# Early-slot transposes three steps later, and early weight splits queued behind the routing of tile 5

## The chip, the cores and the metric

One core of a Trainium2 chip. The metric is the device time of one execution in microseconds (us). Engines are named TensorE (PE), VectorE (DVE), ScalarE (ACT), GpSimd (POOL) and SyncE (SP), as in the profile.

## The reference

Causal attention over 2 x 12 heads of 448 tokens, then a dense feed-forward layer with squared ReLU, then a top-1 mixture of 8 experts:

```python
x = attention(q, k, v)                      # (896, 768)
h = np.maximum(x @ w_in, 0.0); y = h * h @ w_out
yn = y / (norm(y) + 1e-6); en = emb / (norm(emb) + 1e-6)
logits = yn @ en.T / tau; idx = argmax(logits); gate_w = softmax(logits)[idx]
for e in range(8):
    mask = idx == e
    out[mask] = gate_w[mask, None] * (np.maximum(y[mask] @ w1[e], 0) @ w2[e])
```

Everything is float32. A product is made from three: each operand is split in a high part (ScalarE's copy, `mh`, `hi`) and a low part (VectorE's subtraction, `ml`, `lo`), both in a type that TensorE takes at full rate, and high x high, high x low and low x high are added up.

## The kernel before

The program runs in stages: attention; the first dense layer; the second dense layer (`b_tiles`, L484), tile by tile over seven tiles of 128 tokens, with 16 steps `f` each (`wo[f]`, six products of 384 columns); then the experts in *slots*. TensorE's order is written out by hand (`manual_schedule`, L871): work that belongs elsewhere hangs as hooks on steps. The other engines' orders come from a scheduler that goes by priorities; `urgent` (L853) raises the priority of what it wraps.

While tile t runs, its hooks route tile t-1 (`route_tile`, L508). Its parts are separated by `yield`, one per hook: transposes `yt` and their split `yhl`; the logit products `lgt` (two parts); the transposes `lg` of the logits (L535), from which VectorE takes a chain of small operations on 128x8 elements (L542 to L553) to the one-hot mask `OH`; then the rank product `rk` (L556), which reads `OH`. For tile 5, routed during tile 6, `rt6` hangs the parts on steps 1, 4, 7, 9 and 15.

The expert that is most frequent in the first five tiles is known early, and the *early slot* begins with its weights: 16 rows of tiles, loaded in 8 pieces (`pieces`, L663) of two, each split by ScalarE (`mh`) and VectorE (`ml`). Row k overwrites the place of `wo[k]`, so its `mh` waits until TensorE is through with step k of tile 6. The pieces are hooks of tile 6 (`hooks[-1]`): L489 makes one on every even step from 2 on; `all_of(ewl)` (L900) makes the last. Two gathered blocks of early tokens (`xr`) are transposed on steps 10 to 13 (`xe`; `xt`, L837), four groups of three; each group goes to a buffer of the PSUM pool `ps_h` (three buffers, L433, shared with `yt` and the products `hps`) and is emptied by a ScalarE cast (L841) and VectorE's subtraction `act<-xt`.

The early slot then runs `mm1` (8 steps of 18 products, `hps`) and `mm2` for its two halves of 128 tokens (8 steps of six products each, `ops`, L793). Through them goes one more iterator, `first()` (L1055): the routing of tile 6, the tables of all later slots (`tables`, ending in `tabp` and the row indices `fgi`), the gathers of the rows of the next slot M (POOL, L827), and the three groups of transposes of those rows: 128 tokens in two groups, then the remaining 32 tokens in one. `ft0`, `ft1`, `ft2` (L1064) say on which steps of `mm1`, of half 0 and of half 1 it advances. Slot M uses the early slot's weights.

Of the kernel before, what the change touches and what calls it, by code (L numbers as in the profile page):

```python
# [13 lines left out]
ALU = mybir.AluOpType  # L14
# [18 lines left out]
def f32(ap):  # L33
    return ap.bitcast(F32)


CFG = dict(
    first=1, rt5=[1, 3, 4, 5, 8], hp=3000, xe=[1, 10, 11, 12, 13], turn=5, xfd=[3, 4, 5, 6], xfj=[1, 2, 3, 4],
    joint=1, mhi="A", rt6=[1, 4, 7, 9, 15], woh="A", h2h="A", h2l="V", rt=[1, 3, 5, 7, 10], et=[9, 10, 14],
    turn2=[1, 3], ft0=[0, 1, 2, 3, 4], ft1=[3, 7], ft2=[2, 4, 5, 6], stop=0, mlo="V", xh="A", h2="A",  # L40
    wh="G", wil="G", wol="GV", warm=6, nsa=6, nwi=3, nwb=3, wo0=4, hs0=[4, 5, 8, 9], conv0=17, convs=2, pin=1,
    qsb=2, pb=2, ptb=2, qkraw=3, vraw=2, vb=2, ss=4, pts=3, pvs=1, pas=4, wsp=1, mz="G",
    seq=("p0 s0 n0 t0 v0 s1 v1 s2 t1", "n0 t2 s0 v2 v3 t3 s1 s2 w0"),
    ch=(((2, 0, 1), (3,), ()), ((6,), (4, 5), ())), wn=[1], qh="A", qdir=1, qss=2, rpin=5, qdma="SS", kh="V",
    vh="AG", kl="G", vl="G", pth="AAAA", nrm="GGGGGGG", u0=1, order=[2, 1, 3, 0, 4])


def build(tc, qkd, vd, w_in, w_out, emb, tau, wm, cst, out, dbg_y=None):
    nc = tc.nc
    V, A, G, T, DMA = nc.vector, nc.scalar, nc.gpsimd, nc.tensor, nc.sync  # L50
# [14 lines left out]
    def lo_of(eng, lo, x, hi):  # L65
        eng.tensor_tensor(out=lo, in0=x, in1=hi, op=ALU.subtract)  # L66
# [18 lines left out]
    c_tok1, c_im8, c_col, c_lane, c_kc, c_zi, c_ze, c_cap = (  # L85
        c_[k] for k in ("tok1", "im8", "col", "lane", "kc", "zi", "ze", "cap"))
# [42 lines left out]
    last = {}  # L129
# [239 lines left out]
    for p in (ps_v, ps_t, ps_s):  # L369
# [4 lines left out]
    h2 = [h2a_pool.tile([P, NF, GT], F32, tag="h2", name="h2_0"),  # L374
          h2b_pool.tile([P, NF, GT], F32, tag="h2", name="h2_1")]
# [33 lines left out]
    def more_h2():  # L409
        if chunks:  # L410
            c = chunks.pop(0)
            hsd[c] = h2_split(*c)
# [35 lines left out]
    def norm_of(pool, ss, n, name):  # L448

        r = pool.tile([P, 1], F32, tag="nr", name=name + "r")  # L450
        t = pool.tile([P, 1], F32, tag="nt", name=name + "t")
        V.tensor_scalar(out=r[:n].bitcast(I32), in0=ss.bitcast(I32), scalar1=1, scalar2=None,
                        op0=ALU.logical_shift_right)
        V.tensor_scalar(out=r[:n].bitcast(I32), in0=r[:n].bitcast(I32), scalar1=-1.0, scalar2=float(0x5F3759DF),
                        op0=ALU.mult, op1=ALU.add)
        for _ in range(3):
            V.scalar_tensor_tensor(out=t[:n], in0=r[:n], scalar=ss, in1=r[:n], op0=ALU.mult, op1=ALU.mult)
            V.tensor_scalar(out=t[:n], in0=t[:n], scalar1=-0.5, scalar2=1.5, op0=ALU.mult, op1=ALU.add)
            V.tensor_tensor(out=r[:n], in0=r[:n], in1=t[:n], op=ALU.mult)
        V.tensor_tensor(out=t[:n], in0=r[:n], in1=ss, op=ALU.mult)  # L460
        return t

    es = rpool.tile([E, 1], F32, name="es")
# [13 lines left out]
    OH = rpool.tile([P, NTI, E], BF16, name="OH")  # L477
# [6 lines left out]
    def b_tiles(ts, hooks={}):  # L484
        ps = {t: [ps_y.tile([P, 512], F32, tag=f"y{c}", name="yps") for c in range(2)] for t in ts}
        for f in range(NF):
            for x in hooks.get(f, ()):
                next(x, None)
            if f and f % 2 == 0 and -1 in hooks:  # L489
                next(hooks[-1], None)  # L490
            wh, wl = wo[f]
            for t in ts:
                hi, lo = (hsd[t, f // 4][:, i, f % 4, :] for i in range(2))
                for x, w in ((hi, wh), (hi, wl), (lo, wh)):
                    for c in range(2):
                        T.matmul(ps[t][c][:, :384], x, w[:, c * 384:(c + 1) * 384],  # L496
                                 start=(f == 0 and w is wh and x is hi), stop=(f == NF - 1 and x is lo))
            if f % 4 == 3:
                for t in ts:
                    more_h2()  # L500
        ys = {}
        for t in ts:
            ys[t] = bpool.tile([P, DM], F32, tag="ysb", bufs=2, name="ysb")
            for c in range(2):
                A.copy(ys[t][:, c * 384:(c + 1) * 384], ps[t][c][:, :384])
        return ys

    def route_tile(t, y):  # L508
        p0 = t * P
        DMA.dma_start(out=ydram[p0:p0 + P, :], in_=y)  # L510
        lgt = ps_r.tile([2 * E, 2 * P], F32, tag="lg", name="lgt")
        ytt = []
        for c in range(2):
            yt = ps_h.tile([P, 512], F32, tag="h", name="yt")[:, :384].rearrange("p (a b) -> p a b", b=P)
            for j in range(3):
                kc = 3 * c + j
                T.transpose(yt[:, j], y[:, kc * P:(kc + 1) * P], ident)
            ytt.append(yt)
        ss = rpool.tile([P, 1], F32, tag="ss", bufs=2, name="ss")
        sq = spool.tile([P, DM], BF16, tag="relu", name="sq")  # L520
        A.activation(sq, y, AF.Square, accum_out=ss)
        for c in range(2):
            yhl = bpool.tile([P, 3, 2, P], F32R, tag="yhl", name="yhl")
            A.copy(yhl[:, :, 0], ytt[c])
            lo_of(V, yhl[:, :, 1], ytt[c], f32(yhl[:, :, 0]))
            yield
            for j in range(3):
                kc = 3 * c + j
                T.matmul(lgt, ent[:, kc], yhl[:, j].rearrange("p a b -> p (a b)"), start=(kc == 0), stop=(kc == KC - 1))
        lgs = spool.tile([2 * E, 2, P], F32, tag="relu", name="lgs")  # L530
        V.tensor_copy(lgs, lgt.rearrange("p (a b) -> p a b", a=2))
        yield
        lg = ps_r.tile([P, 2, 2 * E], F32, tag="lg", name="lg")
        for j in range(2):
            T.transpose(lg[:, j], lgs[:, j], ident[:2 * E, :2 * E])  # L535
        nrm = norm_of(rpool, ss, P, "yn")
        sc = rpool.tile([P, 1], F32, tag="sc", bufs=2, name="sc")
        V.tensor_scalar(out=sc, in0=nrm, scalar1=1.0e-6, scalar2=None, op0=ALU.add)
        V.reciprocal(sc, sc)
        V.tensor_tensor(out=sc, in0=sc, in1=rtau, op=ALU.mult)  # L540
        l = rpool.tile([P, E], F32, tag="l", bufs=2, name="l")
        V.reduce_sum(out=l, in_=lg.rearrange("p j (a b) -> p b (j a)", b=E), axis=AX.X)  # L542
        V.tensor_scalar(out=l, in0=l, scalar1=sc, scalar2=None, op0=ALU.mult)
        m = rpool.tile([P, 4], F32, tag="m", bufs=2, name="m")
        V.reduce_max(out=m[:, 0:1], in_=l, axis=AX.X)
        V.tensor_scalar(out=m[:, 1:2], in0=m[:, 0:1], scalar1=-1.0, scalar2=None, op0=ALU.mult)
        ex = rpool.tile([P, E], F32, tag="ex", bufs=2, name="ex")
        A.activation(ex, l, AF.Exp, bias=m[:, 1:2], accum_out=m[:, 2:3])

        c8 = rpool.tile([P, E], F32, tag="c8", bufs=2, name="c8")  # L550
        V.scalar_tensor_tensor(out=c8, in0=l, scalar=m[:, 0:1], in1=c_im8, op0=ALU.is_ge, op1=ALU.mult)
        V.tensor_reduce(out=m[:, 3:4], in_=c8, op=ALU.min, axis=AX.X)
        V.tensor_scalar(out=OH[:, t], in0=c_im8, scalar1=m[:, 3:4], scalar2=None, op0=ALU.is_equal)  # L553
        yield
        rk = ps_r.tile([P, E], F32, tag="lg", name="rk")
        T.matmul(rk, tri, OH[:, t], start=True, stop=False)  # L556
        T.matmul(rk, ones, OHs[:, t], start=False, stop=True)
        V.tensor_tensor(out=OHs[:, t + 1], in0=OHs[:, t], in1=OH[:, t], op=ALU.add)

        g = rpool.tile([P, 1], F32, tag="g", bufs=2, name="g")  # L560
        V.tensor_scalar(out=g, in0=m[:, 2:3], scalar1=1.0e-9, scalar2=None, op0=ALU.add)
        V.reciprocal(g, g)
        gh = rpool.tile([P, 1], F32R, tag="gh", bufs=2, name="gh")
        V.tensor_copy(gh, g)
        V.tensor_copy(vals[:, t, 1:2], f32(gh))
        V.tensor_tensor(out=vals[:, t, 2:3], in0=g, in1=f32(gh), op=ALU.subtract)

        V.tensor_tensor(out=c8, in0=rk, in1=OH[:, t], op=ALU.mult)
        V.reduce_sum(out=ranks[:, t:t + 1], in_=c8, axis=AX.X)
# [306 lines left out]
    for t in range(2, NTI):  # L876
        hooks = {}
# [8 lines left out]
        if t == NTI - 1:  # L886
# [4 lines left out]
            ew, ewl = slot_w(eslot)  # L891
# [172 lines left out]
    for i, at in enumerate((CFG["ft0"], CFG["ft1"], CFG["ft2"])):  # L1064
        hooks = {k: [it] for k in at}
# [110 lines left out]
```

## Time and profile before

| | us |
|---|---|
| median of 3 runs | 589.86 |
| lowest, highest | 587.77, 589.89 |
| the profiled execution, its own time | 592.21 |
| its span, first to last instruction | 590.5 |
| TensorE busy in the span | 562.6 (95%) |
| VectorE, ScalarE, GpSimd busy | 399.0, 291.8, 192.3 |
| mean granted TensorE clock | 0.974 of 2.4 GHz |

The span leaves out 1.7 us of the execution around it. Times of rows count from the span's start. A matmul's duration in a row includes the overlap with its neighbours, so the pace of a run of matmuls is read from the starts of the rows.

### The profile page before, as it was taken

The page shows a single profiled execution, that of the slowest core. Times are in us where ns is not written, and L with a number is a line of the kernel's source. Part 1 is how long each engine was busy: PE and PEld are TensorE (multiplying, and loading weights), DVE is VectorE, ACT ScalarE, POOL GpSimd, SP SyncE. Part 2 cuts the span into 40 slices and gives each one's busy share as a digit, 9 for nine tenths or more (in the row PEclk, how much of TensorE's full clock was granted, in tenths as well). Part 3 has the DMA queues.
Part 4 walks back from the last instruction along what each step waited for, and adds up shares of the span by engine and source line. Part 5 has one row for each costly group of instructions (what it writes and reads, how often), then busy time and mean ns, then how long its engine had stood idle before and what let it go on. Part 6 is the DMA issues. An engine that isn't in the chain of part 4 may idle for free.

```text
span 590.5 us, 9782 instructions
## 1 busy us (share of the span) xinstructions
PE 562.6 (95%) x3501; PEld 516.5 (87%) x3501; DVE 399.0 (68%) x901; ACT 291.8 (49%) x654; POOL 192.3 (33%) x204
## 2 busy tenths in 40 slices
PE   6999999999999999999999999797998999899994
PEld 4888788889999999999899999797997788799993
DVE  6878688955687977796654459773187986942741
ACT  4778677523434244425233318511277976823651
POOL 7685667845446543211000010001202711500010
PEclk8899999999999999999999999799999999799998
DMA  7658442323435545341000039006677997950310
GB/s 223 169 144 233 115 99 68 109 85 114 161 123 176 197 162 178 131 175 55 1 27 28 28 110 394 33 1 221 227 221 244 318 340 241 339 182 21 116 44 9
DMA packets 28233, 86.51 MB, mean 147 GB/s; under 512 B 2822, under 2 KB 13062, under 8 KB 28176
## 3 DMA queue, kind: packets, MB, share of 16 engines
q1 hardware_dynamic: 26640, 79.51, 41.4%
q0 software_dynamic: 1536, 6.29, 3.1%
q8 instruction: 29, 0.48, 0.3%
q14 instruction: 28, 0.23, 0.1%
HBM read 75.24 MB, written 6.29 MB: 138 GB/s over the span
## 4 chain that ended last, share of the span: by engine, by line
PE 85%; DVE 6%; DMA 3%; ACT 3%; issue 2%; SPq 0%; POOL 0%; POOLq 0%; DVEq 0%; ACTq 0%
PE yps L496 19%; PE ops L793 9%; PE pa L289 7%; PE pa L290 7%; PE pa L288 7%; PE pv L264 6%; PE s L215 6%; PE pt L247 4%; PE hps L703 3%; DVE ml L66 3%; PE hps L719 2%; PE hps L718 2%; PE ops L735 2%; PE hps L720 2%; PE ops L730 2%
## 5 line engine op out<-in xcount | busy, mean ns | idle before, releaser
L66 DVE TENSOR_TENSOR ml<-xraw,mh 128x768 fp32r<-128x768 f32 x64 | 60.2, 951 | 19.2 <-ACT mh L59 19.0
L59 ACT ACTIVATE mh<-xraw 128x768 fp32r<-128x768 f32 x64 | 53.4, 845 | 19.0 <-PE ops L730 9.9
L215 PE MATMUL s<-kh,q 128*128 128x128 f32 (+6 forms) x168 | 53.4, 352 | 4.4 <-ACT p L219 4.3
L793 PE MATMUL ops<-mh,act 128*128 128x384 f32 x224 | 54.5, 347 | 0.0
L815 POOL DMA_INDIRECT out<-osb,fsi x10 | 24.3, 2433 | 85.5 <-ACT osb L810 63.9
L230 POOL TENSOR_SCALAR p<-p,rs 128x192 f32<-128x192 f32 (+6 forms) x84 | 44.3, 549 | 18.1 <-ACT p L219 11.3
L264 PE MATMUL pv<-pt,v 128*128 128x448 f32 (+7 forms) x288 | 48.6, 303 | 0.2 <-DVE pt L66 0.2
L827 POOL DMA_INDIRECT xr<-ydram,fgi x10 | 14.7, 1467 | 92.3 <-DVE fsi L605 49.8
L219 ACT ACTIVATE p<-s,mn 128x192 f32<-128x192 f32 (+6 forms) x84 | 39.6, 476 | 10.3 <-DVE mn L218 6.0
L123 DVE SCALAR_TENSOR_TENSOR w<-raw,w 128x768 int32<-128x768 int32 x32 | 42.8, 1338 | 0.7
L264 PEld LDWEIGHTS pv<-pt,v 128*128 128x128 f32 (+3 forms) x288 | 36.9, 163 | 5.4 <-issue 0.3
L215 PEld LDWEIGHTS s<-kh,q 128*128 128x128 f32 x168 | 35.4, 215 | 6.5 <-ACT p L219 4.9
L793 PEld LDWEIGHTS ops<-mh,act 128*128 128x128 f32 x224 | 40.2, 192 | 0.8
L66 DVE TENSOR_TENSOR ml<-mraw,mh 128x768 fp32r<-128x768 f32 x32 | 30.1, 950 | 14.8 <-ACT mh L59 14.8
L66 DVE TENSOR_TENSOR hs<-h,hs 128x512 fp32r<-128x512 f32 (+1 forms) x32 | 21.8, 690 | 24.8 <-ACT hs L59 24.6
L218 DVE TENSOR_REDUCE mn<-s 128x1 f32<-128x192 f32 (+6 forms) x84 | 34.1, 413 | 5.0 <-PE s L216 4.6
L121 DVE SCALAR_TENSOR_TENSOR w<-raw,w 128x768 int32<-128x768 int32 x32 | 36.0, 1128 | 0.7
L294 ACT ACTIVATE relu<-pa 128x448 f32<-128x448 f32 x32 | 17.1, 539 | 36.5 <-PE pa L290 36.2
L119 DVE TENSOR_SCALAR w<-raw 128x768 int32<-128x768 int32 x32 | 22.2, 694 | 18.0 <-POOL wi3l L66 6.7
L66 DVE TENSOR_TENSOR pt<-pt 128x512 fp32r<-128x512 f32 x48 | 32.3, 677 | 3.1 <-ACT pt L59 3.1
L247 PE MATMUL pt<-ident,p 128*128 128x128 f32 x192 | 32.1, 284 | 0.0
L59 ACT ACTIVATE mh<-mraw 128x768 fp32r<-128x768 f32 x32 | 26.7, 844 | 9.5 <-PE ops L793 3.7
(457 smaller groups left out, 1664.9 us busy)
## 6 DMA issues: line engine op xcount, KB each, us to landing
xraw<-in_wm SPq DMA_DIRECT2D x32, 768.0 KB, 5.9
raw<-in_w_in SPq DMA_DIRECT2D x16, 768.0 KB, 4.2
raw<-in_w_out SPq DMA_DIRECT2D x16, 768.0 KB, 4.2
mraw<-in_wm SPq DMA_DIRECT2D x16, 768.0 KB, 6.2
qk<-in_qkd SPq DMA_DIRECT2D x11, 448.0 KB, 4.9
q<-qs SPq DMA_DIRECT2D x22, 224.0 KB, 3.9
v<-in_vd SPq DMA_DIRECT2D x12, 256.0 KB, 4.0
ydram<-ysb SPq DMA_DIRECT2D x7, 384.0 KB, 2.3
```

Source lines behind the costliest of these rows:

```text
L59: A.activation(out, in_, AF.Copy, scale=scale)
L66: eng.tensor_tensor(out=lo, in0=x, in1=hi, op=ALU.subtract)
L123: V.scalar_tensor_tensor(out=w[:, x], in0=raw[:, x, 0], scalar=29, in1=w[:, x], op0=ALU.logical_shift_right, op1=ALU.bitwise_or)
L215: T.matmul(ss, d["q2"][:, c, :, :, x].rearrange("p a b -> p (a b)"), d[y][:, :n], start=i == 0, stop=False)
L230: G.tensor_scalar(out=p, in0=p, scalar1=rs[:, COL[c]:COL[c] + 1], scalar2=1.0, op0=ALU.mult, op1=ALU.mult)
L247: T.transpose(pt[:, o * P:(o + 1) * P], d["p"][c][:, j * P:(j + 1) * P], ident)
L264: T.matmul(d["pv"][:, j * P:S] if h else d["pv"][0:D, j * P:S], d[x][0:k, j, 1:3].rearrange("p a b -> p (a b)") if h else d[x][0:k, j, 0], ...
L288: T.matmul(ps, wh[:, c], xhi[:, kc, gs], start=(kc == 0), stop=False)
L289: T.matmul(ps, wh[:, c], xlo[:, kc, gs], start=False, stop=False)
L290: T.matmul(ps, wl[:, c], xhi[:, kc, gs], start=False, stop=(kc == KC - 1))
L496: T.matmul(ps[t][c][:, :384], x, w[:, c * 384:(c + 1) * 384], start=(f == 0 and w is wh and x is hi), stop=(f == NF - 1 and x is lo))
L793: T.matmul(ps[c], x, ww[:, c * 384:(c + 1) * 384], start=(fc == 0 and x is hh and ww is wh), stop=(fc == 7 and x is hl))
```

## The change

Three edits. `ft1` loses its step 7: from there on `first()` advances one hook later each time. A list `ew` gives the steps of tile 6 on which a piece of the early weights is made: 2 and 4 as before, then three pieces on step 10, one on 12, one on 14 (before: 2, 4, 6, 8, 10, 12, 14). And from step 10 on the pieces are traced under `issue_after` the instruction that wrote `OH` last, which is the mask of tile 5; it adds an order edge on that instruction's engine, VectorE, and no semaphore.

```diff
--- before.py
+++ after.py
@@ -37,7 +37,7 @@
 CFG = dict(
     first=1, rt5=[1, 3, 4, 5, 8], hp=3000, xe=[1, 10, 11, 12, 13], turn=5, xfd=[3, 4, 5, 6], xfj=[1, 2, 3, 4],
     joint=1, mhi="A", rt6=[1, 4, 7, 9, 15], woh="A", h2h="A", h2l="V", rt=[1, 3, 5, 7, 10], et=[9, 10, 14],
-    turn2=[1, 3], ft0=[0, 1, 2, 3, 4], ft1=[3, 7], ft2=[2, 4, 5, 6], stop=0, mlo="V", xh="A", h2="A",
+    turn2=[1, 3], ft0=[0, 1, 2, 3, 4], ft1=[3], ft2=[2, 4, 5, 6], ew=[2, 4, 10, 10, 10, 12, 14], stop=0, mlo="V", xh="A", h2="A",
     wh="G", wil="G", wol="GV", warm=6, nsa=6, nwi=3, nwb=3, wo0=4, hs0=[4, 5, 8, 9], conv0=17, convs=2, pin=1,
     qsb=2, pb=2, ptb=2, qkraw=3, vraw=2, vb=2, ss=4, pts=3, pvs=1, pas=4, wsp=1, mz="G",
     seq=("p0 s0 n0 t0 v0 s1 v1 s2 t1", "n0 t2 s0 v2 v3 t3 s1 s2 w0"),
@@ -486,8 +486,12 @@
         for f in range(NF):
             for x in hooks.get(f, ()):
                 next(x, None)
-            if f and f % 2 == 0 and -1 in hooks:
-                next(hooks[-1], None)
+            for _ in range(CFG["ew"].count(f) if -1 in hooks else 0):
+
+                with ExitStack() as es:
+                    if f > CFG["rt6"][3]:
+                        es.enter_context(tc.issue_after(last["oh"].ins))
+                    next(hooks[-1], None)
             wh, wl = wo[f]
             for t in ts:
                 hi, lo = (hsd[t, f // 4][:, i, f % 4, :] for i in range(2))
@@ -550,7 +554,7 @@
         c8 = rpool.tile([P, E], F32, tag="c8", bufs=2, name="c8")
         V.scalar_tensor_tensor(out=c8, in0=l, scalar=m[:, 0:1], in1=c_im8, op0=ALU.is_ge, op1=ALU.mult)
         V.tensor_reduce(out=m[:, 3:4], in_=c8, op=ALU.min, axis=AX.X)
-        V.tensor_scalar(out=OH[:, t], in0=c_im8, scalar1=m[:, 3:4], scalar2=None, op0=ALU.is_equal)
+        last["oh"] = V.tensor_scalar(out=OH[:, t], in0=c_im8, scalar1=m[:, 3:4], scalar2=None, op0=ALU.is_equal)
         yield
         rk = ps_r.tile([P, E], F32, tag="lg", name="rk")
         T.matmul(rk, tri, OH[:, t], start=True, stop=False)
```

VectorE, tile 6, the end of the routing chain of tile 5. Before, from L540 of that chain to the mask:

```order
L540 TENSOR_TENSOR sc<-sc,rtau 128x1
L66 TENSOR_TENSOR ml<-xraw,mh 128x768
L66 TENSOR_TENSOR act<-xt,act 128x3x128
L543 TENSOR_SCALAR l<-l,sc 128x8
L66 TENSOR_TENSOR ml<-xraw,mh 128x768
L545 TENSOR_REDUCE m<-l 128x1
L66 TENSOR_TENSOR ml<-xraw,mh 128x768
L546 TENSOR_SCALAR m<-m 128x1
L551 SCALAR_TENSOR_TENSOR c_4185<-l,m,ct 128x8
L552 TENSOR_REDUCE m<-c_4185 128x1
L561 TENSOR_SCALAR g<-m 128x1
L553 TENSOR_SCALAR OH<-ct,m 128x8
```

With the change, the end of the same chain and what follows the mask (the lines are 4 higher, L557 is the mask):

```order
L555 SCALAR_TENSOR_TENSOR c_4167<-l,m,ct 128x8
L556 TENSOR_REDUCE m<-c_4167 128x1
L565 TENSOR_SCALAR g<-m 128x1
L557 TENSOR_SCALAR OH<-ct,m 128x8
L66 TENSOR_TENSOR ml<-xraw,mh 128x768 x2
L566 RECIPROCAL g<-g 128x1
L66 TENSOR_TENSOR ml<-xraw,mh 128x768
L562 TENSOR_TENSOR OHs<-OHs,OH 128x8
L66 TENSOR_TENSOR ml<-xraw,mh 128x768
L66 TENSOR_TENSOR ml<-mraw,mh 128x768 x2
L66 TENSOR_TENSOR act<-xt,act 128x3x128
L66 TENSOR_TENSOR ml<-mraw,mh 128x768
```

The splits `ml` that stood between the links of the chain now stand behind the mask, six of them ahead of the first `act<-xt`, the copy that empties the first group of early-token transposes.

TensorE, early slot, from the table product on. Before (`xt` 128x128 x3 is the first group of slot M's transposes):

```order
L596 MATMUL tabp<-rv,ol 128x108 x7
L793 MATMUL ops<-mh,act 128x384 x2
L793 MATMUL ops<-ml,act 128x384 x2
L793 MATMUL ops<-mh,act 128x384 x4
L793 MATMUL ops<-ml,act 128x384 x2
L793 MATMUL ops<-mh,act 128x384 x4
L793 MATMUL ops<-ml,act 128x384 x2
L793 MATMUL ops<-mh,act 128x384 x4
L793 MATMUL ops<-ml,act 128x384 x2
L793 MATMUL ops<-mh,act 128x384 x2
L837 MATMUL xt<-ident,xr 128x128 x3
L793 MATMUL ops<-mh,act 128x384 x2
```

With the change, the end of that stretch and the three groups:

```order
L797 MATMUL ops<-mh,act 128x384 x2
L841 MATMUL xt<-ident,xr 128x128 x3
L797 MATMUL ops<-mh,act 128x384 x2
L797 MATMUL ops<-ml,act 128x384 x2
L797 MATMUL ops<-mh,act 128x384 x4
L797 MATMUL ops<-ml,act 128x384 x2
L797 MATMUL ops<-mh,act 128x384 x2
L841 MATMUL xt<-ident,xr 128x128 x3
L797 MATMUL ops<-mh,act 128x384 x2
L797 MATMUL ops<-ml,act 128x384 x2
L797 MATMUL ops<-mh,act 128x384 x2
L841 MATMUL xt<-ident,xr 128x32 x6
```

Between `tabp` and the first group stand 42 products where 24 stood; the second group follows 12 products after the first (18 before), the third 6 after the second (12 before).

## Rows read from the trace of the kernel before

**Rows 1.** The chain that ended last, shares of the span by engine.

```profile
PE 85%; DVE 6%; DMA 3%; ACT 3%; issue 2%; SPq 0%; POOL 0%; POOLq 0%; DVEq 0%; ACTq 0%
```

**Rows 2.** Waits of TensorE, 340 to 425 us: us in total, times, longest.

```profile
PE xt L837 <- DMA xr<-ydram,fgi: 3.3, 1, 3.3
PE rk L556 <- DVE OH L553: 2.8, 1, 2.8
PE tabp L596 <- DVE ol L593: 0.4, 1, 0.4
```

**Rows 3.** TensorE in order of time: start us, us, engine, line, operation, [idle before].

```profile
364.20 0.29 PE L535 MATMUL lg<-ident,lgs 16*128 16x16 f32 x2
...
369.74 0.49 PE L837 MATMUL xt<-ident,xr 128*128 128x128 f32 x3
...
371.83 0.51 PE L496 MATMUL yps<-wo14h,hs 128*128 128x384 f32 x2
375.15 0.17 PE L556 MATMUL rk<-OH,tri 128*128 128x8 bf16 x1 [2.80 <-DVE OH L553]
...
377.72 1.54 PE L517 MATMUL yt<-ident,ysb 128*128 128x128 f32 x6 [0.25 <-ACT ysb L505]
...
382.37 0.51 PE L529 MATMUL lgt<-yhl,ent 128*16 128x256 f32 x3
...
384.82 0.51 PE L529 MATMUL lgt<-yhl,ent 128*16 128x256 f32 x3
...
389.82 0.18 PE L556 MATMUL rk<-OH,tri 128*128 128x8 bf16 x1
```

**Rows 4.** VectorE in order of time, 340 to 381 us.

```profile
340.71 0.19 DVE L542 TENSOR_REDUCE l<-lg 128x8 f32<-128x32 f32 x1
...
342.15 0.22 DVE L553 TENSOR_SCALAR OH<-ct,m 128x8 bf16<-128x8 f32 x1
...
371.80 0.55 DVE L66 TENSOR_TENSOR act<-xt,act 128x384 fp32r<-128x384 f32 x1
372.26 0.22 DVE L543 TENSOR_SCALAR l<-l,sc 128x8 f32<-128x8 f32 x1
372.39 0.95 DVE L66 TENSOR_TENSOR ml<-xraw,mh 128x768 fp32r<-128x768 f32 x1
373.26 0.15 DVE L545 TENSOR_REDUCE m<-l 128x1 f32<-128x8 f32 x1
...
374.88 0.22 DVE L553 TENSOR_SCALAR OH<-ct,m 128x8 bf16<-128x8 f32 x1
...
380.02 0.56 DVE L66 TENSOR_TENSOR yhl<-yt,yhl 128x384 fp32r<-128x384 f32 x1
```

**Rows 5.** Stretches: PE, PEld, DVE, ACT, POOL busy, granted clock, DMA share, GB/s.

```profile
374.90:381.70 6.80, 6.30 (x27) 5.79 (x27) 3.49 (x19) 2.80 (x6) 0.00 (x0) 0.50 0.16 60
...
412.50:415.80 3.30, 3.30 (x12) 3.30 (x11) 0.16 (x1) 1.03 (x2) 1.03 (x1) 0.50 1.02 417
...
504.60:511.40 6.80, 6.60 (x25) 4.62 (x23) 6.12 (x11) 4.76 (x9) 3.76 (x1) 0.50 0.88 321
```

**Rows 6.** The chain in order of time, 404 to 424 us: start, us, what.

```profile
404.77 6.12 DMA xr<-ydram,fgi
...
411.03 0.52 PE xt L837 x3
411.55 4.70 PE ops L793 x18
...
416.58 2.10 PE ops L793 x12
...
423.54 0.15 PE hps L703
```

**Rows 7.** Waits of TensorE from 425 us on.

```profile
PE hps L730 <- DVE hr L774: 2.7, 2, 1.4
```

**Rows 8.** DMA issues, the early tokens' gathers: median us to landing last.

```profile
xr<-ydram,egi POOLq DMA_INDIRECT x2, 8.6
```

## The prediction

> **What bounds the kernel now.** I read the chain of waits first. TensorE carries 85% of it, VectorE 6%, DMA 3% [rows 1]: time is won only where TensorE stands still or runs at its lower clock. So I asked next who TensorE waits for, in the stretch that the diff touches (340 to 425 us: tile 6 of the second dense layer, then the early slot). Two waits matter: 2.80 us for the routing mask `OH` of tile 5, and 3.30 us for the gathered rows `xr` of slot M [rows 2]. Both places then have to be looked at in order of time.
>
> *Wait A.* TensorE reaches the rank product `rk` of tile 5 when step 14 of tile 6 is done, about 372.35, and starts it at 375.15 [rows 3]. VectorE writes `OH` only at 374.88, though the logits it rests on were transposed at 364.20. The reason shows in VectorE's order: between two links of that short chain stands each time a 0.95 us split of an early weight (`ml`), which holds the queue for 0.87 us (372.39 to 373.26) [rows 4]. For tile 4, with nothing between, the same chain took 1.44 us from the reduction `l` at 340.71 to `OH` at 342.15 [rows 4].
>
> *Wait B.* The gather of slot M's rows goes out at 404.77 and takes 6.12 us; its transposes start at 411.03 [rows 6]. TensorE has been idle 3.30 us by then [rows 2].
>
> *The clock.* The table of stretches adds a second price: from 374.9 to 381.7, after wait A, and again from 412.5 to 415.8, after wait B, the granted clock is 0.50 of full, so 1.2 instead of 2.4 GHz, while TensorE is busy for nearly all of both [rows 5]. A third such stretch (504.6 to 511.4) lies in a later slot that the diff does not touch.
>
> **The change, part by part.** No operation is added or removed; the conditional passes at the program's end are ordered a little otherwise, but they do not run with this input.
>
> *1. Early splits behind `OH`.* Pieces 2 and 3 move from steps 6 and 8 to step 10 and, with everything later, get an order edge behind `OH` of tile 5. VectorE then has no split between the second `yhl` and `OH`. The transpose of the logits at 364.20 takes 0.29 us, so `l` can start at about 364.5 and `OH` stands at 364.5 + 1.44 = 365.95, nine microseconds earlier. Wait A itself (2.80) is gone, with 6 us to spare. SP's queue is not passed: pieces 6 and 7 need the splits of pieces 0 and 1, which stay in place.
>
> What is late next is a step that nobody waited for: the copies `act<-xt` that empty the transposes of the early tokens. They now stand behind six `ml` (12 `ml`, 4 `act` and 7 small operations follow `OH` before tile 6's `yhl`). With 0.87 us for an `ml`, 0.46 for an `act` (371.80 to 372.26) and 0.1 for a small one (372.26 to 372.39) [rows 4], the first `act` ends at 366.1 + 6 x 0.87 + 0.2 + 0.55 = 372.1. The PSUM pool `ps_h` has three buffers, so the fourth transpose group, which started at 369.74 [rows 3], must wait for just that copy: a new wait of **2.4 us, two steps earlier**. After it come the transposes (0.25), steps 13 to 15 (18 products at 2.10/12 = 0.175 us [rows 6], 3.15), the copy of `ysb` (0.25), six transposes (0.8, half of the 1.54 at the lower clock) and the first step of the slot's products (384.82 - 382.37 = 2.45 less the `lgt` products 0.35, so 2.1 [rows 3]). At the full clock that gives 372.15 + 0.25 + 3.15 + 0.25 + 0.8 + 2.1 = 378.7 for the first `lgt` of tile 6, which was at 382.37. But `lgt` reads `yhl`, and VectorE reaches it after 12 x 0.87 + 4 x 0.46 + 7 x 0.1 + 0.3 = 13.3 us, at 379.4, done at 379.95. So the gain of this part is at most 382.37 - 380.0 = 2.4 us.
>
> Its size hangs on the clock. Waits of 2.80 and 3.30 us were each followed by the lower level [rows 2, 5]; 2.4 us is nearer to these than to the other waits of the stretch, none over 0.4 [rows 2]. I take it that the clock falls, once, for the shorter of the two lengths seen (3.3 us shown, half of it lost: 1.7), since this time 3.4 us of work without a gap follow. Then step 15 ends at 375.55 + 1.7, the six transposes start at 377.5, and `yhl` is done 2.86 us later as before (377.72 to 380.58 [rows 3, 4]): `lgt` at 380.4 to 380.7. **Part 1: 1.7 us**, with ends 2.4 (no fall) and 0.3 (lower level over all of the 3.4 us of work: 372.15 + 6.8 + 3.15 = 382.1).
>
> The Trainium skill has a rule here (TensorE: Matmul & The Clock Gate, "Why this matters for your kernels"): it warns of idle gaps between bursts of matmuls, and the gap that it names is longer than wait A. By the page neither wait A nor the new 2.4 us would cost the clock; the row after wait A says otherwise [rows 5], and I follow the row. By the page part 1 would give 2.4 and the kernel would come out at 582.8.
>
> *2. Slot M's transposes later.* Dropping the step at 7 in the first half moves them from (half 0, step 7), (half 1, 2) and (half 1, 4) to steps 2, 4 and 5 of half 1. Where TensorE stood it now runs three steps, 18 products of 0.175 = 3.15 us; 0.15 of the 3.30 us wait is left. Waits that short were not followed by a lower clock [rows 2, 5], so that loss goes too: the 18 products behind the landing took 4.70 us at the lower level, against 3.15, so 1.55 us. Slot M's first product, at 423.54 [rows 6], comes 3.15 + 1.55 earlier. **Part 2: 4.7 us**, with ends 4.9 (nothing of the wait left) and 3.15 (rival three).
>
> The gather itself moves along with the ranks: from the rank product of tile 6 to the gather the chain is VectorE's, and neither its operations nor the DMAs around it change (SP's prefetch and POOL's gather are both released by the same table). Three steps stand between the last transposes and slot M's first product, 3.15 us, for a copy and a subtraction of about 0.5 each (`act`, 0.55 [rows 4]), so nothing new waits there. The scatter of the first half's rows waits for nothing later than before.
>
> Behind 425 us TensorE's longest single wait is 1.4 us [rows 7]; weights there are freed by TensorE's own progress, so the rest should shift as a block.
>
> *Sum.* 1.7 + 4.7 = 6.4 us. Against the profiled execution's own 592.21 that is 585.8; that execution is 2.35 us above the median of the timed runs, 589.86, from which I forecast **583.5 us**. A measurement of this kernel tells about 0.5% (2.9 us) from no change.
>
> **The rivals.**
> - *The new wait does not lower the clock* (it is the shortest of the three): part 1 gives 2.4, total 7.1, 582.8. For it: 2.4 is less than any wait that was followed by a fall. Chance 0.15.
> - *The new waits eat part 1.* The wait at the fourth transposes and the lower clock behind it, lasting as long as the 6.8 us after wait A, leave 0.3: total 5.0, 584.9. For it: a gap at `ysb` stood in the longer stretch too, and it stays. Chance 0.17.
> - *The gather lands later.* The two earlier gathers, under the same load of weight DMAs, took 8.6 us instead of 6.1 [rows 8]. Then 2.6 us of wait B and its clock loss stay: part 2 gives 3.15, total 4.85, 585.0. Chance 0.1.
> - *Given back later.* Slot M starts 5 us sooner after its weights' prefetch went out; if the next slot's splits or DMAs, not TensorE, set the pace there, most of it returns: 587 to 590. Against it: TensorE's waits there are short [rows 7]. Chance 0.07.
> - *Slower.* One mechanism could do it: the clock falls at the new wait and does not come back during the early slot's first four steps, because TensorE keeps meeting VectorE (fourth transposes, `ysb`, `yhl`). The 14 us of work from 372.15 to the rank product of tile 6 (0.25 + 3.15 + 0.8 + 4 x 2.45) would take 28, so `rk` comes near 400.5 instead of 389.82 [rows 3]: 10.7 lost, 4.7 won, 596. It decides if the level is still 0.50 where it had returned before (381.7) [rows 5]. Dense steps brought it back then, so chance 0.03.
>
> **How the numbers follow.** The forecast has 0.48. All but the last two cases lie within 582.8 to 585.0; the timed runs themselves spread over 2.1 us, and the third low-clock stretch (6.8 us, half lost) may come or go. That gives 580.0 to 587.6, which leaves out the slower case and the worse half of the one before it. Faster by over 0.5% (under 586.9): the forecast, three rivals and part of the fourth, less the spread, 0.86; within 0.5%: 0.11; slower: 0.03.
>
> **What would show it right or wrong.** `OH` of tile 5 near 366 and no wait at its `rk`; a wait of 2 to 2.8 us for VectorE's `act` at the fourth early transposes, near 370; the first `lgt` of tile 6 near 380.5; TensorE's wait for `xr` down to under 0.5 us, and no 0.50 stretch behind it; from the rank product of tile 6 to slot M's first product 4.7 us less than before. A gather that takes 8 us, a 0.50 stretch over the early slot's products, or new waits for VectorE or ACT in the next slot would each break a step of this.

## The result, and the profile after

The changed kernel took **585.70 us** (median of 8 runs, 583.95 to 586.50), the kernel before beside it 589.88 us (median of 8, 587.77 to 593.03). The ratio on record is 0.9911, with a 95% interval of 0.9889 to 0.9932: faster by 0.9%, or 5.2 us. It is not the quotient of the two medians: these lie 4.2 us apart. So gains in time are given both ways below, by the ratio and by the medians. The forecast was 583.5 us, with a range of 580.0 to 587.6.

The profiled execution of the changed kernel took 583.95 us, its span is 582.2 us. That of the kernel before had 592.21 [rows 1 to 8 are from it], so the pair that is compared below lies 8.3 us apart, well over the 4.2 us between the medians. That difference has to be explained too.

The chain that ended last has hardly other shares than before [rows 1]:

```profile
PE 85%; DVE 5%; DMA 4%; ACT 3%; issue 2%; SPq 1%; POOL 0%; POOLq 0%; ACTq 0%
```

TensorE's waits from 340 to 425 us (total, times, longest) answer to [rows 2]. Both large ones are gone, and there is one new one of 2.1 us:

```profile
PE xt L841 <- DVE act L66: 2.1, 1, 2.1
PE yt L521 <- ACT ysb L509: 0.4, 1, 0.4
PE lgt L533 <- DVE yhl L66: 0.4, 1, 0.4
PE tabp L600 <- DVE ol L597: 0.4, 1, 0.4
PE cnt L913 <- DVE c L572: 0.3, 1, 0.3
```

TensorE in order of time (start, us, line, operation, idle before), as [rows 3]. Lines from 491 on stand four higher than before:

```profile
364.28 0.29 PE L539 MATMUL lg<-ident,lgs 16*128 16x16 f32 x2
...
372.07 0.55 PE L841 MATMUL xt<-ident,xr 128*128 128x128 f32 x3 [2.08 <-DVE act L66]
...
374.57 0.18 PE L560 MATMUL rk<-OH,tri 128*128 128x8 bf16 x1
...
376.33 0.93 PE L521 MATMUL yt<-ident,ysb 128*128 128x128 f32 x6 [0.39 <-ACT ysb L509]
...
379.72 0.53 PE L533 MATMUL lgt<-yhl,ent 128*16 128x256 f32 x3 [0.35 <-DVE yhl L66]
...
387.19 0.18 PE L560 MATMUL rk<-OH,tri 128*128 128x8 bf16 x1
...
415.70 0.31 PE L707 MATMUL hps<-act,mh 128*128 128x320 f32 x1
```

The first `lgt` of tile 6 comes 379.72 - 364.28 = 15.44 us after the `lg` transposes of tile 5, where it was 382.37 - 364.20 = 18.17 [rows 3]. VectorE shows why (as [rows 4]): `OH` stands at 366.2, then six splits run before the first copy `act<-xt`, and `yhl` comes after all of them:

```profile
365.99 0.22 DVE L557 TENSOR_SCALAR OH<-ct,m 128x8 bf16<-128x8 f32 x1
366.12 1.82 DVE L66 TENSOR_TENSOR ml<-xraw,mh 128x768 fp32r<-128x768 f32 x2
...
369.73 1.82 DVE L66 TENSOR_TENSOR ml<-mraw,mh 128x768 fp32r<-128x768 f32 x2
371.46 0.55 DVE L66 TENSOR_TENSOR act<-xt,act 128x384 fp32r<-128x384 f32 x1
...
379.12 0.55 DVE L66 TENSOR_TENSOR yhl<-yt,yhl 128x384 fp32r<-128x384 f32 x1
```

The stretches (us, then busy time of PE, PEld, DVE, ACT and POOL, granted clock, DMA share, GB/s), as [rows 5]. Behind the new wait and over slot M's transposes the clock is full; two shorter stretches at 0.50, 1.2 GHz, lie in later slots:

```profile
374.50:381.50 7.00, 6.25 (x50) 5.55 (x49) 6.71 (x21) 4.57 (x10) 0.00 (x0) 1.00 0.16 61
...
408.00:415.70 7.70, 7.70 (x51) 7.35 (x49) 1.47 (x3) 1.28 (x3) 2.37 (x3) 1.00 1.02 391
450.30:453.60 3.30, 3.25 (x14) 2.32 (x12) 3.30 (x8) 2.73 (x6) 3.30 (x1) 0.50 0.85 290
498.10:501.40 3.30, 3.30 (x13) 2.36 (x12) 3.30 (x7) 2.46 (x6) 2.55 (x1) 0.50 0.94 292
```

The chain from the table's products to slot M's first product, as [rows 6]. The transfer `xr` has left the chain; the 18 products that ran behind its landing for 4.70 us now run ahead of the transposes, among the 42:

```profile
399.88 0.99 PE tabp L600 x7
400.87 7.36 PE ops L797 x42
408.23 0.33 PE xt L841 x3
408.57 2.09 PE ops L797 x12
410.65 0.33 PE xt L841 x3
410.98 1.06 PE ops L797 x6
412.04 0.48 PE xt L841 x6
412.52 3.33 PE ops L797 x18
415.86 0.15 PE hps L707
```

From the rank product of tile 6 to slot M's first product it is 415.86 - 387.19 = 28.67 us, where it was 423.54 - 389.82 = 33.72 [rows 3, 6]: 5.05 less. (In the chain slot M's first product starts 0.16 us later than in the order of time, 415.86 against 415.70; the table below takes the order of time, so it has 28.51 and 33.56.)

### The profile page after: what moved, and what is told of

The parts are those of the page before. It is cut to its first block, busy times and chain, and to the rows that moved or that the text cites. A ratio compares the mean times of both kernels' runs of the same rounds, so it can differ in the third digit from the quotient of the medians.

```text
span 582.2 us, 9781 instructions
## 1 busy us (share of the span) xinstructions
PE 558.6 (96%) x3501; PEld 512.2 (88%) x3501; DVE 399.6 (69%) x901; ACT 291.5 (50%) x654; POOL 188.3 (32%) x204
## 4 chain that ended last, share of the span: by engine, by line
PE 85%; DVE 5%; DMA 4%; ACT 3%; issue 2%; SPq 1%; POOL 0%; POOLq 0%; ACTq 0%
PE yps L500 19%; PE ops L797 10%; PE pa L290 7%; PE pa L289 7%; PE pa L288 7%; PE pv L264 6%; PE s L215 5%; PE pt L247 3%; PE hps L707 3%; DMA q<-qs 3%; PE ops L739 3%; PE ops L734 2%; DVE ml L66 2%; PE hps L723 2%; PE hps L722 2%
## 5 line engine op out<-in xcount | busy, mean ns | idle before, releaser
L831 POOL DMA_INDIRECT xr<-ydram,fgi x10 | 10.7, 1067 | 89.3 <-DVE fsi L609 47.1
L59 ACT ACTIVATE pt<-pt 128x512 fp32r<-128x512 f32 x48 | 28.1, 599 | 5.9 <-PE pt L247 3.8
```

The source lines that it names most:

```text
L59: A.activation(out, in_, AF.Copy, scale=scale)
```

## Experiments

A total time mixes the stretch that the change touches with 360 us ahead of it and 165 us behind it. So each profile was also cut at four places of TensorE's order of time: `lg` of tile 5, the first `lgt` of tile 6, the rank product of tile 6, and slot M's first product. Each number is a difference of two starts in one profiled execution; the last column is the span less the start of slot M's first product. The runs stand under the names of their labels and are explained below.

| profile | lg to lgt | lgt to rank | rank to M | lg to M | M to the end |
|---|---|---|---|---|---|
| before | 18.17 | 7.45 | 33.56 | 59.18 | 167.1 |
| before_2 | 18.20 | 7.45 | 33.52 | 59.17 | 167.5 |
| before_3 | 18.13 | 7.47 | 31.66 | 57.26 | 166.3 |
| splits_only | 15.43 | 7.56 | 33.30 | 56.29 | 166.2 |
| splits_only_2 | 15.44 | 7.47 | 33.18 | 56.09 | 166.3 |
| splits_only_3 | 16.49 | 7.47 | 33.37 | 57.33 | 166.0 |
| transposes_only | 16.78 | 7.44 | 28.65 | 52.87 | 167.4 |
| transposes_only_2 | 17.09 | 7.45 | 28.74 | 53.28 | 168.6 |
| after | 15.44 | 7.47 | 28.51 | 51.42 | 166.5 |
| after_again | 16.52 | 7.47 | 28.84 | 52.83 | 167.5 |
| after_3 | 15.44 | 7.47 | 28.64 | 51.55 | 167.5 |
| act_first | 15.18 | 7.46 | 28.64 | 51.28 | 167.5 |
| defer | 12.67 | 8.99 | 28.04 | 49.70 | 166.0 |
| defer_late | 12.67 | 7.46 | 28.73 | 48.86 | 168.7 |

### The changed kernel and the kernel before, again

No edit: these runs show what differs from one execution to the next. Expected of the changed kernel, in the first group of runs and in the last:

> The changed kernel once more, as a yardstick. Two readings of the gap between the profiled pair (8.3 us) and the medians (4.2 us). Theory C: the waits are the same in every execution, and where the clock falls to 0.50 differs; then the waits here stand as in the first profile to 0.1 us (fourth early transposes 2.1, yt 0.4, lgt 0.4, none for OH or xr), the stretches at 0.50 are others, and the time stays within 583.9 to 587. Rival G: the gather of slot M's rows lands at other times; then the wait for xr differs from run to run by 0.5 us or more.

> The changed kernel a third time. Theory C: part 1 and part 2 add up to 6.4 us by the stretches (58.5 us from lg of tile 5 to slot M's first product in the mean of three profiles before, 52.1 in two after), so 584 if the kernel before is at 590.4; the two timings so far gave 4.2 and 4.8 us, with intervals that reach to 6.5 and 6.3. If the difference to the transposes alone is under 0.5 us again, part 1 is not worth its 1.7 us in the time.

Measured: 586.58 us (9 runs) against 590.53, ratio 0.9919 (0.9893 to 0.9945), and 586.79 us (7 runs) against 590.72, ratio 0.9919 (0.9886 to 0.9953): 4.8 us twice by the ratios, 4.0 and 3.9 by the medians. The 584 us that theory C gave for after_3 did not come. The wait at the fourth early transposes is 2.1 us again in both; the first has 0.2 us at `xr` and none at `lgt`. So of the two readings theory C holds: the waits stay and the clock differs. In after_again alone of the three the wait of 2.1 us was followed by the lower clock, and the first `lgt` came 1.1 us later for it. The stretch of after_again:

```profile
373.10:376.40 3.30, 3.30 (x12) 3.30 (x13) 3.30 (x6) 1.03 (x2) 0.00 (x0) 0.50 0.00 0
```

Expected of the kernel before:

> The kernel before once more, for its profile. Theory C (how long the clock stays low after a wait differs between executions): the waits are 2.8 us for OH and 3.2 to 3.3 us for xr again, both are followed by a stretch at 0.50, but the one after OH is not always 6.8 us; where it is 3.4 us, the first lgt of tile 6 comes 16.8 us after the lg transposes of tile 5 and not 18.2. Rival (the long stretch belongs to the kernel): 6.8 us again, and 18.2.

> The kernel before a third time: as for the second. From the lg transposes of tile 5 to slot M's first product 56.8 to 59.2 us, less the shorter the low stretch after OH is; from the rank product of tile 6 to slot M's first product 33.3 to 33.6 us each time.

Measured: 592.89 and 589.13 us, one execution each. Theory C failed for the wait for `OH`: 6.8 us at the lower clock all three times, and 18.1 to 18.2 us. For the wait for `xr` the length did not change, but the third profile has no fall at all: 31.66 us from the rank product to slot M, outside the 33.3 to 33.6 expected of it and 1.9 less than in the other two. Some 1.6 of these are the clock and the rest the wait itself, 3.0 us against 3.3 and 3.2. The waits of before_3, its stretch around that wait, and its chain (the 18 products take 3.14 us, against 4.70 [rows 6]):

```profile
PE xt L837 <- DMA xr<-ydram,fgi: 3.0, 1, 3.0
PE rk L556 <- DVE OH L553: 2.8, 1, 2.8
```

```profile
374.60:381.20 6.60, 6.09 (x26) 5.59 (x26) 3.33 (x18) 2.79 (x6) 0.00 (x0) 0.50 0.16 62
409.00:416.00 7.00, 5.61 (x35) 5.61 (x36) 1.11 (x2) 2.01 (x4) 2.00 (x2) 1.00 1.02 384
```

```profile
404.46 5.79 DMA xr<-ydram,fgi
...
410.91 3.14 PE ops L793 x18
```

before_3 has no low stretch around 505 us either. It is the fastest of the three; the two slower ones hold all three low stretches [rows 5].

### Each part alone

The edits against the changed kernel; only the entries of `CFG` and the line that change are shown:

```diff
 # splits_only, splits_only_2, splits_only_3
-    ft1=[3], ew=[2, 4, 10, 10, 10, 12, 14]
+    ft1=[3, 7], ew=[2, 4, 10, 10, 10, 12, 14]
 # transposes_only, transposes_only_2
-    ft1=[3], ew=[2, 4, 10, 10, 10, 12, 14]
+    ft1=[3], ew=[2, 4, 6, 8, 10, 12, 14]
...
-                    if f > CFG["rt6"][3]:
+                    if False:
```

> Only the splits of the early weights are moved behind the routing mask; slot M's transposes stand where they stood before. The prediction's part 1: 1.7 us, so 588.2 against 589.9. Theory C (a wait lowers the clock in some executions only): the wait of 2.80 us is exchanged for 2.1 + 0.4 us and what the clock loses is a matter of the execution, so 0.4 to 1.5 us, 588.4 to 589.5. Both: TensorE waits about 3.3 us for xr, the wait for OH is gone, and the fourth early transposes wait 2.1 us. If more than 2.6 us come out, the splits carry more than the prediction gave them.

> The splits alone once more, for a second profile. Theory C: the wait of 2.1 us at the fourth early transposes lowers the clock in some executions, in one of the three seen so far; lgt comes 15.4 us after lg of tile 5 without a fall, 16.5 with one. The wait for xr is 3.2 us and is followed by 3.4 us at 0.50. Rival (the wait of 2.1 us costs the clock by its place or its load): the same every time.

> The splits alone, timed a second time. By the stretches of the two profiles so far the first lgt of tile 6 comes 15.4 us after lg of tile 5 where the kernel before has 18.1 to 18.2, so 2.7 us are won there; where the wait of 2.1 us is followed by the lower clock (it was in one of four profiles) 1.65. Theory C then has the time 1.6 to 2.7 us under the kernel before's. Rival B (given back behind slot M's first product, or lost ahead of tile 6): the same stretch is 2.7 us shorter, but the time within 1 us of the kernel before, as the first timing had it (0.9995).

Measured: 589.61 us (12 runs) against 590.53, ratio 0.9995 (0.9974 to 1.0016), and 589.93 us (12 runs) against 590.72, ratio 0.9981 (0.9957 to 1.0006); splits_only_2 is one execution of 587.20 us. In time the splits give 0.3 and 1.1 us by the ratios, 0.9 and 0.8 by the medians, and neither is told from nothing. That is what rival B of the third expectation had for the time, within about 1 us of the kernel before, and less than the 1.6 to 2.7 of theory C. From `lg` to the first `lgt` they give 2.7 us twice and 1.7 once, when the 2.1 us wait was followed by the lower clock. The two large waits of splits_only:

```profile
PE xt L841 <- DMA xr<-ydram,fgi: 3.2, 1, 3.2
PE xt L841 <- DVE act L66: 2.1, 1, 2.1
```

> Only slot M's transposes are moved three steps on; the splits of the early weights stand where they stood before. The prediction's part 2: 4.7 us, so 585.2 against 589.9. Theory C: the 3.15 us of wait are won in every execution, the 1.55 us of clock only where it had fallen, so 3.1 to 4 us, 585.9 to 586.8. Both: the wait for OH stays at 2.8 us, the wait for xr falls under 0.3 us. A theory of interplay (the two parts win the same time) would have it give all 4.2 us and the splits nothing.

> The transposes alone, timed a second time, beside the whole change on the same chip. The prediction's part 2: 4.7 us under the kernel before's. By the profiles so far 4.9 us where the wait for xr was followed by the lower clock (two of three profiles of the kernel before), 3.0 where it was not. In the profile the clock falls behind the wait of 2.8 us for OH, as it did all four times.

Measured: 585.90 us (6 runs), ratio 0.9925 (0.9897 to 0.9953), and 586.83 us (12 runs), ratio 0.9927 (0.9905 to 0.9950): 4.4 and 4.3 us by the ratios, 4.6 and 3.9 by the medians, close to the 4.7 of the prediction's part 2. No wait for `xr` is left over 0.1 us, the wait for `OH` stays, and the lower clock behind it lasted 3.4 us instead of 6.8, though no instruction up to that place stands in another order than in the kernel before. So the first `lgt` came 1.1 to 1.4 us sooner after `lg` than in the kernel before, and that is not a gain of this edit by its order; whether it is chance, two profiles don't show. The wait and the two stretches of transposes_only:

```profile
PE rk L560 <- DVE OH L557: 2.8, 1, 2.8
```

```profile
375.00:378.30 3.30, 3.05 (x12) 2.54 (x12) 0.38 (x5) 1.69 (x4) 0.00 (x0) 0.50 0.01 2
378.50:385.50 7.00, 7.00 (x61) 6.79 (x60) 4.96 (x21) 2.12 (x6) 0.00 (x0) 1.00 0.13 49
```

By the ratios the parts add up: 0.7 (mean of 0.3 and 1.1) and 4.35 make 5.05, and the whole change gave 5.2, 4.8 and 4.8. By the medians they make 5.1, and the whole gave 4.2, 4.0 and 3.9. In the stretch the theory of interplay falls: the splits win ahead of the first `lgt`, the transposes behind the rank product, and the changed kernel has both (15.44 and 28.51). In time it is not ruled out. On the same chips the whole change had 586.58 us against 585.90 for the transposes alone, and 586.79 against 586.83; by the ratios it is 0.4 and 0.5 us ahead. That is the case for which the expectation of after_3 said that part 1 is not worth its 1.7 us in the time.

### What the new wait stands for

Here every split from row 4 of the early weights on has an order edge of its own, on VectorE's low part. Pieces are issued at the steps of `ew`; `xa0` to `xa3` are the copies of the early tokens, `yhl0` and `yhl1` those of tile 6, `sc` and `lgs` the steps of the routing, `ol` the mask of the last table. Only the lines that place the splits are shown:

```diff
+                pin = CFG["pins"].get(k) if s[3] is ear["eidx"] else None
+                with tc.issue_after(last[pin].ins) if pin else ExitStack():
-                lo_of(ENG[CFG["mlo"][k % len(CFG["mlo"])]], lo, x, f32(hi))
+                    lo_of(ENG[CFG["mlo"][k % len(CFG["mlo"])]], lo, x, f32(hi))
 # act_first: ew=[2, 4, 10, 11, 12, 13, 14]
+    pins={4: "oh", 5: "oh", 6: "xa0", 7: "xa0", 8: "xa1", 9: "xa1", 10: "xa2", 11: "xa2",
+          12: "xa3", 13: "xa3", 14: "xa3", 15: "xa3"}
```

> As the changed kernel, but each of the four copies of the early tokens goes ahead of the splits that stood before it on VectorE; the number of splits ahead of the second yhl is the same. Theory D (what holds TensorE here is the sum of VectorE's work from OH to yhl, 12 splits and 4 copies, some 13 us): the wait at the fourth early transposes goes, and TensorE waits about 2 us at lgt for yhl instead; the first lgt of tile 6 starts at 379.5 to 380 as in the changed kernel, and the time is 585.7 within 1 us. Rival Q (the order in the queue is what costs): no wait comes back, the first lgt starts near 377.6 and the time is 2.1 us less, 583.6.

Measured: 584.70 us (6 runs), ratio 0.9889 (0.9856 to 0.9921), which overlaps with the changed kernel's 0.9919 (0.9893 to 0.9945) on the same chip. In time it lies 1.8 us under the changed kernel there (1.9 by the medians), nearer to the 2.1 of rival Q than to theory D, but with these intervals the time tells neither. The profile does, and theory D holds: TensorE no longer waits for the copies, it waits at `lgt` instead. The first `lgt` moves by 0.26 us (15.18 against 15.44), not by 2.1, and slot M by as little (51.28 us after `lg`; the changed kernel without a fall of the clock has 51.42 and 51.55). The waits of act_first and that row in order of time:

```profile
PE lgt L533 <- DVE yhl L66: 1.7, 1, 1.7
PE hps L722 <- DVE act L66: 0.4, 1, 0.4
```

```profile
381.06 0.52 PE L533 MATMUL lgt<-yhl,ent 128*16 128x256 f32 x3 [1.69 <-DVE yhl L66]
```

So work has to leave the stretch, not change places in it. Pieces 4 to 7 belong to the slot's second layer, which starts some 20 us after the first; some of their splits can wait. (In defer_late the low part of the last row is, besides, made only at step 3 of half 0; those lines are not shown.)

```diff
 # defer: ew=[2, 4, 10, 11, 12, 13], the last two pieces at steps 1 and 3 of the slot's first layer
+    pins={4: "sc", 5: "oh", 6: "oh", 7: "xa0", 8: "xa0", 9: "xa1", 10: "xa1", 11: "xa2",
+          12: "xa3", 13: "yhl0", 14: "yhl1", 15: "sc"}
 # defer_late: ew=[2, 4, 10, 11, 12, 13, 14], the last piece at step 1
+    pins={4: "yhl1", 5: "lgs", 6: "oh", 7: "oh", 8: "xa0", 9: "xa0", 10: "xa1", 11: "xa1",
+          12: "xa2", 13: "xa3", 14: "yhl0", 15: "ol"}
```

> As the changed kernel, but the sixteen early splits are spread: one ahead of the reduction of tile 5's logits, the copies of the early tokens ahead of the splits, and the last three behind yhl of tile 6, since only eight of the sixteen are needed by the slot's first products. Theory D (VectorE's sum from OH to yhl is what TensorE waits for): with four splits less ahead of the second yhl and three less ahead of the first, neither the fourth early transposes nor lgt wait over 0.5 us, the first lgt comes 13 to 13.6 us after lg of tile 5 where the changed kernel has 15.4, and the time is 1.8 to 2.4 us under the changed kernel's, near 583.5 to 584 (0.989 of the kernel before or less). Rival S (the spread splits hit the routing of tile 6 instead): the rank product of tile 6 comes over 8.3 us after the first lgt instead of 7.5, or slot M's first product later than 28.6 us behind it, and half or all is given back.

Measured: 582.73 us (6 runs) against 590.45, ratio 0.9879 (0.9860 to 0.9897): 7.1 us by the ratio, 7.7 by the medians. The first `lgt` comes 12.67 us after `lg`, 2.8 less than in the changed kernel and sooner than the 13 to 13.6 expected. Rival S was right too: the split behind `sc` stands ahead of the scaling of the logits `l`, holds up the routing of tile 6, and its rank product waits. VectorE of defer in order of time, and TensorE's wait:

```profile
382.98 0.15 DVE L544 TENSOR_TENSOR sc<-sc,rtau 128x1 f32<-128x1 f32 x1
383.05 0.95 DVE L66 TENSOR_TENSOR ml<-xraw,mh 128x768 fp32r<-128x768 f32 x1
383.92 0.23 DVE L547 TENSOR_SCALAR l<-l,sc 128x8 f32<-128x8 f32 x1
```

```profile
PE rk L560 <- DVE g L566: 1.3, 1, 1.3
```

Of the 1.5 us lost there 0.5 come back before the table: its products start 12.18 us behind the ranks, where the changed kernel has 12.69. The last kernel keeps the routing free:

> As the deferred splits, but none stands in the routing of tile 6: two ahead of the reduction of tile 5's logits, eight between OH and yhl, one behind the first yhl, and the last behind the mask ol, where VectorE waits 1.1 us for the table's products. Theory D: the first lgt 12.7 us after lg of tile 5 as with the deferred splits, the rank product of tile 6 7.5 us later instead of 9.0 and no wait of 1.3 us there, slot M's first product 48.5 to 49 us after lg of tile 5 (deferred 49.7, changed kernel 51.4 to 52.8), and the time about 1 us under the deferred splits', 581.5 to 582.5. Rival S (the last split delays the table's copy, the gather lands later): the wait for xr grows by 0.5 us or more and the gain is gone.

Measured: **582.43 us** (5 runs) against 590.72, ratio **0.9843 (0.9810 to 0.9877)**, 9.3 us less than the kernel before (8.3 by the medians); the changed kernel on the same chip has 0.9919 (0.9886 to 0.9953), so the two intervals do not touch. From `lg` to slot M it takes 48.86 us, no wait in the stretch is over 0.4 us, and the last split fits where VectorE waits for the table's products. VectorE of defer_late, in order of time:

```profile
397.19 1.08 DVE L597 TENSOR_TENSOR ol<-ct,lane 128x896 fp32r<-128x896 f32 x1
398.19 0.95 DVE L66 TENSOR_TENSOR ml<-xraw,mh 128x768 fp32r<-128x768 f32 x1
399.36 0.27 DVE L603 COPY ftab<-tabp 128x108 f32<-128x108 f32 x1 [0.21 <-PE tabp L600]
```

Of the two deferred versions the stretch tells them apart (49.70 and 48.86); the intervals of their times overlap.

## Why the prediction was right, and where it was off

**The mechanisms stood as forecast.** `OH` was forecast for 365.95 and was written from 365.99; its wait is gone. The copy `act<-xt` that frees the third buffer was forecast to end at 372.1 and ended at 371.46 + 0.55 = 372.01; the wait it causes was forecast at 2.4 us, two steps earlier than wait A, and is 2.08. The first `lgt` was forecast for 379.95 to 380.0 without a fall of the clock, and came at 379.72; with one, for 380.4 to 380.7, so 16.2 to 16.5 us after `lg`, and came 16.5 us after it in after_again and splits_only_3. What holds it is VectorE's sum, as the prediction had it ("VectorE reaches it after 12 x 0.87 + 4 x 0.46 + ..."): act_first shows it, and the deferred versions turn it into a gain.

**Part 2 was right in size.** 4.7 us forecast, 4.4 and 4.3 in time with the part alone (4.6 and 3.9 by the medians), 4.9 in the stretch where the clock had fallen behind the wait for `xr` (33.5 to 28.65), 3.0 where it had not (31.66 to 28.65). The lower end of 3.15 us was named as the case of a late gather; it belongs to executions without the fall. The rival of a late gather itself did not come: no profile with the moved transposes has a wait for `xr` over 0.2 us.

**The case taken as likeliest at the new wait was the rarer one.** Of six profiles with that wait the clock fell behind it in two. So the rival "does not lower the clock" described most of them.

**The term that was off is part 1, as a gain in time.** It stood in the sum with 1.7 us. In the stretch it was there: 2.0 us from `lg` to slot M in the mean of the splits alone. In time the splits alone gave 0.3 and 1.1 us, and on top of the transposes 0.4 and 0.5 by the ratios and none by the medians. So of the 6.4 us forecast 5.2 came (4.2 by the medians), and what is missing is missing mainly here. A part of it shows in the table: in the two profiles of the transposes alone the wait for `OH` cost less than in the three of the kernel before (3.4 us at the lower clock, not 6.8), so that on top of them the splits win only 1.1 us from `lg` to slot M (53.1 against 51.9 in the mean).

**What was luck, and what stays a suspicion.** Against the profiled execution's own 592.21 the sum gave 585.8, and the changed kernel's median is 585.70; that closeness is luck, since part 1 did not come out so. The forecast itself subtracted the sum from the median, "that execution is 2.35 us above the median of the timed runs, 589.86, from which I forecast 583.5 us". One can suspect that a loss was counted twice there: of the three profiles of the kernel before, 592.21 and 592.89 us have a fall behind the wait for `xr` and another near 505 us, 589.13 has neither. But that is not shown. Five of the six profiles that wait for `xr` have the fall, and part 2 alone, measured against medians, gave nearly all of its 4.7 us.

**Some of it may have been given back, by the clock.** From slot M's first product to the end the six profiles that still wait for `xr` take 166.6 us in the mean, the eight without that wait 167.5. Five of these eight have a stretch at 0.50 near 450 us, in the slot after M, as the changed kernel's at 450.3, and all eight one near 500 us; of the six none has the first and three have the second. The time behind slot M goes with this: the five profiles with at most 3.4 us at 0.50 between slot M's first product and 520 us take 166.0 to 166.3, those with 6.8 us 166.5 to 167.5, with 10.2 us 167.5, with 13.7 us 168.6 and 168.7. TensorE's longest wait there is the same in all fourteen, 1.4 us for `hr`, as in [rows 7]; the row of the changed kernel:

```profile
PE hps L734 <- DVE hr L778: 2.7, 2, 1.4
```

That would put some 0.9 us on the rival "given back later", by the clock and not by splits or DMAs; the prediction had the clock there only as a spread ("may come or go"). It is a difference of means over few profiles, and between the three of the kernel before and the three of the changed kernel alone it is only 0.2 (167.0 and 167.2).

**What stays open.** By the stretch from `lg` to slot M the change wins 58.5 - 51.9 = 6.6 us (means of three profiles each), by the time 4.8 to 5.2, or 3.9 to 4.2 by the medians. The same six profiled executions differ by 5.6 us in their own times: 0.8 of the 6.6 are lost ahead of `lg` (364.2 against 365.0 us) and 0.2 behind slot M's first product. Up to 360 us no engine's order differs between any two of the kernels, yet the fourteen profiles reach `lg` anywhere from 363.0 to 365.9 us, and the first product of the first dense layer at 112.2 to 115.5 us already. The rest may lie in that spread, or the profiled executions of the kernel before, 591.4 us in the mean against a median of 590.5, are again not the typical ones. The runs don't settle it. The two intervals for part 1 reach from 0.9 us lost to 1.5 won and from 0.4 lost to 2.5 won, so that the prediction's 1.7 lies outside one and inside the other. The rival that "the new waits eat part 1" has, with 5.0 us, the total closest to the 5.2 by the ratio; but the lower clock for 6.8 us, which was to cause it, was in none of the six profiles with the new wait.

## What to carry to other kernels

When a wait for a queue is taken away by a new order in the queue, add up all that the queue must do before the *next* operand that the bound engine needs: if that sum does not fall, the wait comes back under another name, and only work that leaves the stretch wins time. Before a loss that is read from one profiled execution goes into a sum, profile the same kernel again: here one of three executions had no lower clock behind the wait for `xr`, and the part was worth 3.0 us in it and not 4.9. And where a total carries noise from parts that the change doesn't touch, cut every profile at the same three or four instructions: here such a difference agreed to 0.2 us between executions of a kernel in which the clock fell at the same places, while the totals of one kernel varied by 3 us and more.

## What the runs showed of the hardware

The lower clock after a wait of TensorE is a matter of the execution, for the same instructions. In the fourteen profiles it followed the 2.8 us wait for `OH` five times in five (for 6.8 us three times, for 3.4 twice), the wait of 3.0 to 3.3 us for `xr` five times in six (always for 3.4 us), and the 2.1 us wait at the fourth early transposes two times in six (for 3.4 us). It did not follow the 1.7 us wait of act_first or the 1.3 us wait of defer. Near 450 us it fell behind waits of no more than 1.4 us, in five profiles of fourteen that all have this wait. In one of the two profiles of the transposes alone the fall counted to the wait for `OH` came only some 2 us after TensorE had taken up work again, 0.3 us behind the next wait (0.39 us, for `ysb`). The granted clock was 0.50 in all these stretches, 1.2 instead of 2.4 GHz.

The Trainium skill (TensorE: Matmul & The Clock Gate, "Why this matters for your kernels") warns of idle gaps between bursts of matmuls; the gap that it names is longer than 2.8 us. Here the rows disagree: a gap of 2.8 us was followed by the lower clock every time, and gaps of 2.1 and 1.4 us in some profiles. What lengthens or shortens the low stretch from one execution to the next, no run here shows.

What a fall costs depends on what else TensorE waits for. Behind the wait for `xr` 3.4 us at the lower clock cost some 1.6 us: the 18 products took 4.70 us against 3.14, and of two executions that both waited 3.0 us, splits_only_2 with a fall and before_3 without, one took 33.18 us to slot M and the other 31.66. Ahead of the first `lgt`, where VectorE's splits hold TensorE anyway, a fall of the same length behind the 2.1 us wait cost 1.1 (16.5 against 15.44): the wait of 0.4 us for `yhl` is gone in the profiles with the fall.
